# An RWKV attention and MLP kernel: small matmuls moved to quarters of the TensorE array, and a state without zero blocks

## The chip, the cores and the metric

The kernel runs on one core of a Trainium2 chip. The core has a matrix engine (TensorE, PE in the profile, with its weight loads listed as PEld), VectorE (DVE), ScalarE (ACT), GpSimd (POOL) and SyncE (SP), which issues all of this kernel's data transfers. The metric is device time of one execution in microseconds; lower is better.

TensorE multiplies a stationary operand, which is loaded into the array first, with a moving operand that streams through it. The array has 128 rows (the contraction) and 128 columns (the output's partitions). An operand that is smaller can use a part of it: the row part follows from the partitions on which the operands lie, the column part from the output's partitions. The profile writes this as rows*columns: `64*128` is a half with 64 rows, `128*64` a half with 64 columns, `64*64` a quarter.

## The reference

An RWKV-6 attention with a decay of its own for every step and channel, then an MLP with a squared ReLU. Batch 4, 8 heads, 768 steps, head size 48; model size 384, hidden size 2048. All inputs and the output are float32.

```python
for t in range(S):
    cur = np.einsum('bhd,bhe->bhde', u[None] * kt, vt)
    y[:, :, t] = np.einsum('bhd,bhde->bhe', rt, state + cur)
    state = wt[:, :, :, None] * state + np.einsum('bhd,bhe->bhde', kt, vt)
...
x = attn_out.transpose(0, 2, 1, 3).reshape(B * S, H * D)
h = x @ w_in
out = np.maximum(h, 0.0) ** 2 @ w_out
```

## The kernel before

**Tiling.** The sequence of a batch is cut into three steps of 256 positions, so there are 12 steps `s`. A step holds two chunks `c` of 128 positions. Partition `c*64 + p` holds positions `2p` and `2p+1` of chunk `c`; the two are called `j` = 0 and 1. The 8 heads go in 4 pairs `p`, with `e` = 0 or 1 for the head in the pair. A head's 48 channels are padded to 64, so that a pair fills 128 partitions after a transpose.

**Attention in a step.** `ww_`, `lw_`, `cum_`, `exp_` build the decays; `ac_` (L298) writes each chunk's whole decay to `ac_buf`; `rd_` (L305) multiplies r and k by decays into `rdec_buf`; `tr_` and `rkt_` transpose them on TensorE into `rkT`, or `dtr_` does it by a DMA. Then:

- `p_` (L341): scores of a chunk, k against r, 32 matmuls on 64x64 quarters of the array, one for each pair, chunk, head and `js`; `pm_` (L351, L354) masks them into `pmT`.
- `su_` (L371): what a chunk adds to the state, k times v. A matmul takes two heads at once, 128 columns by 96, so half of its output is a product of one head's k with the other head's v and is not wanted.
- `ts_` (L379, L381): adds the old state to it, from PSUM to `t_state`, 384 elements a partition, on DVE or ACT.
- `sn_` (L386): multiplies by the chunk's decay on POOL and writes the new bf16 state `S`. Its factor `ac_buf` holds zeros for the unwanted head of each partition, so the unwanted blocks of `S` become zero.
- `y_` (L408): masked scores times v, 32 matmuls of 48 columns with 64 rows and 128 columns of the array.
- `yq_` (L416): adds the bonus term. `vq` (v times a scalar for each position and head, made by `vq_` on POOL) is added through `spread`, an identity put in one half of 128 columns for each `j`.
- `yc_` (L422): r times the carried state, 128 rows by 64 columns of the array, 96 columns of `S` for a head pair. The zero blocks let one matmul serve two heads. In a batch's first step the first chunk has no state to carry.
- `ysb_` and `yt_`/`xt_` or `dyt_`: copy y out of PSUM and transpose it for the MLP.

`y_`, `yq_` and `yc_` accumulate in the same two PSUM banks, one for each chunk `c`, through the helper `y_mm` (L394), which is why all three have line L394 in the profile. `yy_(s)` runs `su_(s+1)`, `y_(s)`, `yq_(s)`, `yc_(s)` in a row on TensorE. In a batch's last step `su_` makes the first chunk's part alone.

**MLP.** `m1_` (L464): 6 matmuls of 256 columns for each of 8 groups; `rl_` (L473, L475) takes the ReLU; `sq_` (L481, L483) squares; `m2_` (L489): 16 matmuls of 384 columns for each chunk; `os_` (L496, L498) and `store` bring the result out.

**Order.** The order on every engine is written out by hand in the string `ORDER` (L17 to L86): each word names an operation, its step, the PSUM bank after a colon and the engine after `=` (V is DVE, A is ACT, G is POOL). Every engine runs its part of that list in order. The MLP of earlier steps is interleaved with the attention of later ones. TensorE begins with `warm_` matmuls, whose results are not used, and `constants()` (L210) fills masks, `ident`, `spread` and the zeros of `ac_buf` and `lw_buf`, mostly on POOL.

## Time and profile before

| | |
|---|---|
| three executions | 188.93, 189.06, 189.28 us; median 189.06 |
| span of the profiled execution, first to last instruction | 186.7 us; its own whole time is not listed apart from the three |
| PE busy | 177.0 us, 2303 matmuls |
| DVE, ACT, POOL busy | 125.8, 125.1, 104.9 us |
| `m1_`, L464 | 576 matmuls, 74.3 us |
| `m2_`, L489 | 384 matmuls, 71.9 us |
| `su_`, L371 | 160 matmuls of 96 columns, 6.2 us |
| `y_`, L394 | 384 of 48 columns, 7.1 us |
| `yq_`, L394 | 48 of 384 columns, 6.0 us |
| `yc_`, L394 | 160 of 96 columns, 5.7 us |
| `p_`, L341 | 384 of 128 columns on quarters, 8.2 us |
| `ts_` on DVE, L381 | 16 of 546 ns |
| `sn_` on POOL, L386 | 20 of 935 ns, median 836 |
| `ac_` on ACT, L298 | 24 of 173 ns |

Matmuls are pipelined and those on different parts of the array overlap, so a group's time is best read from the starts of its first matmul and of the next group's. "Idle" in the profile is time in which an engine had nothing running, with the instruction that ended it; "issue" is time in which it waited for nothing that the profile shows. The granted clock of TensorE was 0.999 of full speed.

### The profile page before, as it was taken

The numbers are of one execution on the slowest core, as the hardware profiler recorded it, in microseconds if no ns is written. First come the engines' busy times: TensorE is split into PE (matmuls) and PEld (weight loads), VectorE is DVE, ScalarE is ACT, GpSimd is POOL, SyncE is SP. The second block draws the span as 40 slices with busy tenths as digits, with TensorE's granted clock in tenths as the row PEclk, the third lists the DMA queues.
The fourth block names the chain that finished last, engine by engine and source line by source line (L and its number), as shares of the span: only waits on it lengthen the run. The fifth ranks groups of instructions, "written<-read, shape, count | busy, mean of one in ns | idle before, by whom it ended". The sixth has DMA issues, their size and how long they took to land.

```text
span 186.7 us, 5422 instructions
## 1 busy us (share of the span) xinstructions
PE 177.0 (95%) x2303; PEld 125.4 (67%) x2303; DVE 125.8 (67%) x170; ACT 125.1 (67%) x205; POOL 104.9 (56%) x99
## 2 busy tenths in 40 slices
PE   7686998999999999999999999999999999999992
PEld 2344587766777777777776766777666777776761
DVE  4379979686799876983849699795946472562020
ACT  5278978889659795797687577968541656156732
POOL 7289627695897998959496981563934130000000
PEclk9999999999999999999999999999999999999999
DMA  6999999999999999979999999890539150203022
GB/s 151 269 274 341 330 280 381 340 280 264 275 234 218 257 239 236 248 148 147 279 185 260 220 270 251 240 147 32 66 63 201 30 172 0 46 0 126 4 84 84
DMA packets 78952, 35.81 MB, mean 192 GB/s; under 512 B 72144, under 2 KB 77392, under 8 KB 78928
## 3 DMA queue, kind: packets, MB, share of 16 engines
q1 hardware_dynamic: 78928, 35.46, 82.5%
q8 instruction: 18, 0.29, 0.7%
q14 instruction: 6, 0.05, 0.1%
HBM read 25.36 MB, written 4.72 MB: 161 GB/s over the span
## 4 chain that ended last, share of the span: by engine, by line
PE 80%; DVE 8%; ACT 5%; issue 3%; DMA 3%; SPq 0%; ACTq 0%
PE m L464 32%; PE bk L489 31%; PE att L394 8%; DVE rdec_buf L305 4%; PE att L341 3%; PE att L371 3%; DMA w_raw<-in_w_dram 3%; PE bk L444 1%; PE att L286 1%; PE att L287 1%; ACT att L291 1%; DVE r_raw L256 1%; ACT ac_buf L298 1%; DVE pmT L351 1%; DVE pmT L354 1%
## 5 line engine op out<-in xcount | busy, mean ns | idle before, releaser
L464 PE MATMUL m<-xT,wi_sb 128*128 128x256 bf16 x576 | 74.3, 273 | 0.5 <-ACT gt L473 0.5
L489 PE MATMUL bk<-wo_sb,gt 128*128 128x384 bf16 x384 | 71.9, 326 | 0.0
L464 PEld LDWEIGHTS <-wi_sb 128*128 128x128 bf16 x576 | 54.9, 98 | 13.9 <-issue 1.4
L473 ACT ACTIVATE gt<-m 128x512 f16<-128x512 f32 x68 | 39.7, 596 | 34.4 <-PE m L464 34.1
L489 PEld LDWEIGHTS <-gt 128*128 128x128 bf16 x384 | 36.9, 98 | 19.3
L481 ACT ACTIVATE gt<-gt 128x1024 bf16<-128x1024 f16 x36 | 37.6, 1053 | 0.9 <-DVE gt L475 0.7
L354 DVE TENSOR_TENSOR pmT<-att,mask 128x1024 bf16<-128x1024 f32 x22 | 26.3, 1218 | 5.6 <-PE att L341 5.5
L386 POOL TENSOR_TENSOR S<-t_state,ac_buf 128x384 bf16<-128x384 f32 x20 | 18.7, 935 | 19.9 <-DVE t_state L381 13.2
L475 DVE TENSOR_SCALAR gt<-m 128x512 f16<-128x512 f32 x28 | 19.2, 687 | 14.6 <-PE m L464 11.9
L264 POOL TENSOR_TENSOR ku<-k_raw,u_bc 128x768 f32<-128x768 f32 x12 | 22.5, 1878 | 9.1 <-DVE q L273 4.7
L269 POOL TENSOR_TENSOR ku<-ku,r_raw 128x768 f32<-128x768 f32 x12 | 22.9, 1910 | 1.0 <-DMA r_raw<-in_r_dram 0.8
L277 POOL TENSOR_TENSOR vq<-v_raw,q 128x768 bf16<-128x768 f32 x12 | 18.2, 1520 | 9.1 <-DVE q L273 4.8
L305 DVE TENSOR_TENSOR rdec_buf<-r_raw,att 128x768 bf16<-128x768 f32 x12 | 11.3, 952 | 3.8 <-ACT att L291 2.2
L498 DVE TENSOR_SCALAR o_sb<-bk 128x384 f32<-128x384 f32 x11 | 6.1, 551 | 11.0 <-PE bk L489 11.0
L291 ACT ACTIVATE att<-att 128x768 f32<-128x768 f32 x12 | 9.4, 795 | 3.7 <-PE att L287 3.6
L305 DVE TENSOR_TENSOR rdec_buf<-k_raw,att 128x768 bf16<-128x768 f32 x12 | 11.4, 947 | 0.5 <-ACT ac_buf L298 0.5
L506 PE MATMUL bk<-warm 128*128 128x512 bf16 x35 | 10.5, 452 | 1.2 <-DVE half_ones L212 1.2
L273 DVE TENSOR_REDUCE q<-ku 128x16 f32<-128x768 f32 x12 | 11.3, 943 | 0.0
L496 ACT ACTIVATE o_sb<-bk 128x384 f32<-128x384 f32 x13 | 6.4, 490 | 6.2 <-PE bk L489 6.2
L483 DVE TENSOR_TENSOR gt<-gt 128x1024 bf16<-128x1024 f16 x12 | 8.9, 753 | 2.0 <-ACT gt L473 2.0
L381 DVE TENSOR_TENSOR t_state<-S,att 128x384 f32<-128x384 bf16 x16 | 8.7, 546 | 1.8 <-PE att L371 1.8
L247 ACT ACTIVATE lw_buf<-ww 128x384 bf16<-128x384 f32 x12 | 6.2, 524 | 5.3 <-DVE ww L243 5.3
(72 smaller groups left out, 179.8 us busy)
## 6 DMA issues: line engine op xcount, KB each, us to landing
w_raw<-in_w_dram SPq DMA_DIRECT2D x12, 384.0 KB, 5.1
k_raw<-in_k_dram SPq DMA_DIRECT2D x12, 384.0 KB, 6.1
r_raw<-in_r_dram SPq DMA_DIRECT2D x12, 384.0 KB, 6.2
v_raw<-in_v_dram SPq DMA_DIRECT2D x12, 384.0 KB, 6.0
out_dram<-o_sb SPq DMA_DIRECT2D x24, 192.0 KB, 3.1
w_st<-in_moe_w_in_dram SPq DMA_DIRECT2D x4, 768.0 KB, 8.5
w_st<-in_moe_w_out_dram SPq DMA_DIRECT2D x4, 768.0 KB, 8.7
rkT<-rdec_buf SPq DMA_TRANSPOSE x16, 4.0
```

The costliest lines, as they stand in the source:

```text
L264: nc.gpsimd.tensor_mul(ku[:], raw["k", s][:, :, 1:3, :], u_bc[:, :, None, :].to_broadcast([C, H, 2, D]))
L269: nc.gpsimd.tensor_mul(ku[:], ku[:], raw["r", s][:, :, 0:2, :])
L277: nc.gpsimd.tensor_mul(vq[:].rearrange("p j h d -> p h j d"), raw["v", s][:], tiles.pop(("q", s))[:, :, :, None].to_broadcast([C, H, 2, D]))
L305: nc.vector.tensor_mul(rdec[:, i, :, :, 0:D], x.rearrange("p h j d -> p j h d"), cs[:, i, 0:DM].rearrange("p (h d) -> p h d", h=H)[:, None ...
L354: nc.vector.tensor_mul(pmT, ps_p[:].rearrange("p e (a x) -> p (e a) x", a=2), mk.to_broadcast([C, 4, 2 * C]))
L386: nc.gpsimd.tensor_mul(t[:], tiles.pop(("ts", s, c))[:].rearrange("p (a e d) -> p a e d", a=HP, e=2), tiles["a_c", s][:, :, c, :, None].to ...
L394: nc.tensor.matmul(ps_y[rows, c, cols], lhsT, rhs, start=fresh, stop=True, skip_group_check=True)
L464: nc.tensor.matmul(ps1[:, j, :], wi_sb[:, n // 4, kk, n % 4 * 128:(n % 4 + 1) * 128], tiles["xT", s][:, :, kk, :], start=(kk == 0), stop=( ...
L473: nc.scalar.activation(rl, m1, AF.Relu, scale=RS)
L475: nc.vector.tensor_scalar(out=rl, in0=m1, scalar1=RS, scalar2=0.0, op0=ALU.mult, op1=ALU.max)
L481: nc.scalar.activation(gt, rl, AF.Square)
L489: nc.tensor.matmul(m2, gt[:, n, c * C:(c + 1) * C], wo_sb[:, n, :], start=(n == 0), stop=(n == NT - 1))
```

## The change

- The state has 48 columns for a head pair instead of 96: partitions 0 to 63 hold head `e` = 0 of each pair, 64 to 127 head `e` = 1, and there are no zero blocks. `t_state` and `S` are half as wide, `ac_buf` too; it needs no zeros, and `ac_` is one activation on all 128 partitions.
- `su_` makes one matmul for each head, on a quarter of the array: rows by chunk `c`, columns by `e`, 48 columns moving. 32 matmuls instead of 16.
- `y_` splits its 128 output positions into `j` = 0 and 1, each on a quarter: 64 matmuls instead of 32, still 48 columns.
- `yq_` uses quarters of `ident` for `spread`, which is gone: 4 matmuls with a different quarter each, 384 columns.
- `yc_` makes a matmul for each head. First the half with `e` = `c`, on quarters: 16 matmuls of 48 columns. Then the half with `e` = 1 - `c`, on tiles of 64 rows and 32 columns of the array: 32 matmuls of 48 columns. In the first half, as in `y_`, rows from half `c` of the array write chunk `c`'s bank; in the second they write the other one.
- `ORDER` is unchanged. PE gets 3167 matmuls instead of 2303.

```diff
-    spread = consts.tile([C, 2, C], BF16)
...
-    ac_bufs = [consts.tile([C, HP, 2, 2], FP32, name=f"ac_buf{i}") for i in range(NAC)]
+    ac_bufs = [consts.tile([C, HP, 2], FP32, name=f"ac_buf{i}") for i in range(NAC)]
...
-        for t in ac_bufs:
-            nc.gpsimd.memset(t[:], 0.0)
-        nc.gpsimd.memset(spread[:], 0.0)
         for c in range(2):
             rows = slice(c * Q, (c + 1) * Q)
-            for j in range(2):
-                nc.gpsimd.tensor_copy(spread[rows, j, j * Q:(j + 1) * Q], ident[rows, rows])
...
-        for e in range(2):
-            rows = slice(e * DP, (e + 1) * DP)
-            nc.scalar.activation(
-                a_c[rows, :, :, e], cs[rows, 0, DM:DM + 2 * HP].rearrange("p (a c) -> p a c", c=2), AF.Exp)
+        nc.scalar.activation(a_c[:], cs[:, 0, DM:DM + 2 * HP].rearrange("p (a c) -> p a c", c=2), AF.Exp)
...
-                    part = slice(c * Q, (c + 1) * Q)
-                    nc.tensor.matmul(ps_su[c][:, p * 2 * D:(p + 1) * 2 * D],
-                                     rdec[part, 1, j, 2 * p:2 * p + 2, :], v_bf[part, 2 * p:2 * p + 2, j, :],
-                                     start=(j == 0 and p == 0), stop=(j == 1), skip_group_check=True)
+                    for e in range(2):
+                        part, rows, h = slice(c * Q, (c + 1) * Q), slice(e * DP, (e + 1) * DP), 2 * p + e
+                        nc.tensor.matmul(ps_su[c][rows, p * D:(p + 1) * D], rdec[part, 1, j, h, :],
+                                         v_bf[part, h, j, :], start=(j == 0 and p == 0), stop=(j == 1),
+                                         skip_group_check=True)
...
-        ts = tiles["ts", s, c] = a_mid.tile([C, DM], FP32, name="t_state")
+        ts = tiles["ts", s, c] = a_mid.tile([C, HP * D], FP32, name="t_state")
...
-        t = tiles["S", s + c, 1 - c] = a_mid.tile([C, HP, 2, D], BF16, name="S", bufs=6)
+        t = tiles["S", s + c, 1 - c] = a_mid.tile([C, HP, D], BF16, name="S", bufs=6)
...
+    def y_mm(s, c, rows, cols, lhsT, rhs):
+        fresh = (s, c, rows.start // Q) not in begun
+        begun.add((s, c, rows.start // Q))
+        nc.tensor.matmul(tiles["y", s][rows, c, cols], lhsT, rhs, start=fresh, stop=True, skip_group_check=True)
...
-                        y_mm(s, c, slice(h * D, (h + 1) * D),
-                             pmT[part, p // 2, 2 * e + p % 2, js, :], v_bf[part, h, js, :])
+                        for j in range(2):
+                            rows = slice(j * Q, (j + 1) * Q)
+                            y_mm(s, c, rows, head(h), pmT[part, p // 2, 2 * e + p % 2, js, rows], v_bf[part, h, js, :])
...
-        for j in range(2):
-            for c in range(2):
-                part = slice(c * Q, (c + 1) * Q)
-                y_mm(s, c, slice(0, DM), spread[part, j], vq[part, j].rearrange("p h d -> p (h d)"))
+        for c in range(2):
+            part = slice(c * Q, (c + 1) * Q)
+            for j in range(2):
+                y_mm(s, c, slice(j * Q, (j + 1) * Q), slice(0, DM), ident[part, part],
+                     tiles["vq", s][part, j].rearrange("p h d -> p (h d)"))
...
-        for c in range(0 if s % NB else 1, 2):
-            for p in range(HP):
-                for j in range(2):
-                    y_mm(s, c, slice(2 * p * D, (2 * p + 2) * D),
-                         tiles["rkT", s][:, 0, j, p, c * Q:(c + 1) * Q],
-                         tiles["S", s, c][:, p].rearrange("p e d -> p (e d)"), j)
+        rT = tiles["rkT", s][:, 0]
+        for e_is_c, n in (True, Q), (False, Q // 2):
+            for p in range(HP):
+                for c in range(0 if s % NB else 1, 2):
+                    e = c if e_is_c else 1 - c
+                    rows = slice(e * DP, (e + 1) * DP)
+                    for j in range(2):
+                        for t0 in range(0, Q, n):
+                            y_mm(s, c, slice(j * Q + t0, j * Q + t0 + n), head(2 * p + e),
+                                 rT[rows, j, p, c * Q + t0:c * Q + t0 + n], tiles["S", s, c][rows, p, :])
```

More of the change, by code (lines that the diff above doesn't have):

```diff
@@ L369, in su_ @@
                 for c in range(n_c):
-                    part = slice(c * Q, (c + 1) * Q)
-                    nc.tensor.matmul(ps_su[c][:, p * 2 * D:(p + 1) * 2 * D],
-                                     rdec[part, 1, j, 2 * p:2 * p + 2, :], v_bf[part, 2 * p:2 * p + 2, j, :],
-                                     start=(j == 0 and p == 0), stop=(j == 1), skip_group_check=True)
+                    for e in range(2):
[3 more added lines that the diff above has]
+                                         skip_group_check=True)
     def ts_(s, c):
-        ps_su = tiles["su", s][c][:, 0:DM]
-        ts = tiles["ts", s, c] = a_mid.tile([C, DM], FP32, name="t_state")
+        ps_su = tiles["su", s][c][:, 0:HP * D]
+        ts = tiles["ts", s, c] = a_mid.tile([C, HP * D], FP32, name="t_state")
         if s % NB == 0 and c == 0:
@@ L380, in ts_, with head @@
         else:
-            nc.vector.tensor_add(ts[:], tiles["S", s, c][:].rearrange("p a e d -> p (a e d)"), ps_su)
+            nc.vector.tensor_add(ts[:], tiles["S", s, c][:].rearrange("p a d -> p (a d)"), ps_su)
     def sn_(s, c):
-        t = tiles["S", s + c, 1 - c] = a_mid.tile([C, HP, 2, D], BF16, name="S", bufs=6)
-        nc.gpsimd.tensor_mul(t[:], tiles.pop(("ts", s, c))[:].rearrange("p (a e d) -> p a e d", a=HP, e=2),
-                             tiles["a_c", s][:, :, c, :, None].to_broadcast([C, HP, 2, D]))
-    def y_mm(s, c, cols, lhsT, rhs, j=None):
-        ps_y = tiles["y", s]
-        rows = slice(0, C) if j is None else slice(j * Q, (j + 1) * Q)
-        fresh = (s, c) not in begun
-        begun.add((s, c))
-        nc.tensor.matmul(ps_y[rows, c, cols], lhsT, rhs, start=fresh, stop=True,
-                         skip_group_check=True)
-    begun = set()
+        t = tiles["S", s + c, 1 - c] = a_mid.tile([C, HP, D], BF16, name="S", bufs=6)
+        nc.gpsimd.tensor_mul(t[:], tiles.pop(("ts", s, c))[:].rearrange("p (a d) -> p a d", a=HP),
+                             tiles["a_c", s][:, :, c, None].to_broadcast([C, HP, D]))
+    begun = set()
+    def head(h):
+        return slice(h * D, (h + 1) * D)
+    def y_mm(s, c, rows, cols, lhsT, rhs):
+        fresh = (s, c, rows.start // Q) not in begun
+        begun.add((s, c, rows.start // Q))
+        nc.tensor.matmul(tiles["y", s][rows, c, cols], lhsT, rhs, start=fresh, stop=True, skip_group_check=True)
     def y_(s):
@@ L407, in y_ @@
                         part = slice(c * Q, (c + 1) * Q)
-                        y_mm(s, c, slice(h * D, (h + 1) * D),
-                             pmT[part, p // 2, 2 * e + p % 2, js, :], v_bf[part, h, js, :])
+                        for j in range(2):
+                            rows = slice(j * Q, (j + 1) * Q)
+                            y_mm(s, c, rows, head(h), pmT[part, p // 2, 2 * e + p % 2, js, rows], v_bf[part, h, js, :])
     def yq_(s):
-        vq = tiles.pop(("vq", s))
-        for j in range(2):
-            for c in range(2):
-                part = slice(c * Q, (c + 1) * Q)
-                y_mm(s, c, slice(0, DM), spread[part, j], vq[part, j].rearrange("p h d -> p (h d)"))
+        for c in range(2):
[3 more added lines that the diff above has]
+                     tiles["vq", s][part, j].rearrange("p h d -> p (h d)"))
     def yc_(s):
-        for c in range(0 if s % NB else 1, 2):
+        rT = tiles["rkT", s][:, 0]
+        for e_is_c, n in (True, Q), (False, Q // 2):
             for p in range(HP):
-                for j in range(2):
-                    y_mm(s, c, slice(2 * p * D, (2 * p + 2) * D),
-                         tiles["rkT", s][:, 0, j, p, c * Q:(c + 1) * Q],
-                         tiles["S", s, c][:, p].rearrange("p e d -> p (e d)"), j)
+                for c in range(0 if s % NB else 1, 2):
[5 more added lines that the diff above has]
+                                 rT[rows, j, p, c * Q + t0:c * Q + t0 + n], tiles["S", s, c][rows, p, :])
     def yy_(s):
```

## Prediction

> **What bounds the kernel now.** I read the page's totals first, then the chain of work that ended last, then busy time by stage, then the timeline of one attention step on TensorE (PE).

> ```profile
> PE 177.0 (95%) x2303; PEld 125.4 (67%) x2303; DVE 125.8 (67%) x170; ACT 125.1 (67%) x205; POOL 104.9 (56%) x99
> ...
> PE 80%; DVE 8%; ACT 5%; issue 3%; DMA 3%; SPq 0%; ACTq 0%
> PE m L464 32%; PE bk L489 31%; PE att L394 8%; DVE rdec_buf L305 4%; PE att L341 3%; PE att L371 3%; DMA w_raw<-in_w_dram 3%; PE bk L444 1%; PE att L286 1%; PE att L287 1%; ACT att L291 1%; DVE r_raw L256 1%; ACT ac_buf L298 1%; DVE pmT L351 1%; DVE pmT L354 1%
> ```

> PE is busy for 95% of the span and holds 80% of the chain. The lines that change, L394 and L371, hold 11%, about 20 us; that is all there is to win or multiply. By stage:

> ```profile
> 0.00:20.00 20.00, 14.85 (x176) 7.55 (x176) 13.28 (x22) 12.05 (x25) 14.67 (x30) 1.00 1.01 263
> 20.00:33.00 13.00, 12.43 (x190) 9.44 (x187) 11.69 (x19) 10.78 (x17) 6.49 (x6) 1.00 1.08 333
> 33.00:60.00 27.00, 26.86 (x384) 19.39 (x382) 20.91 (x29) 21.58 (x34) 22.08 (x17) 1.00 1.18 267
> 60.00:90.00 30.00, 30.00 (x433) 22.17 (x432) 23.05 (x31) 23.05 (x41) 25.86 (x21) 1.00 1.02 215
> ```

> PE is the second column. From 33 us on it never really rests, with DVE and ACT (fourth and fifth) at 77%. So PE's own time is the price there, and only before 33 us do other engines set the pace. One attention step (columns: start, length, line, output<-inputs, shapes, count):

> ```profile
> 83.45 0.51 PE L371 MATMUL att<-v_bf,rdec_buf 64*128 64x96 bf16 x16
> 83.80 0.56 PE L394 MATMUL att<-v_bf,pmT 64*128 64x48 bf16 x32
> 84.20 0.48 PE L394 MATMUL att<-vq,spread 64*128 64x384 bf16 x4
> 84.62 0.53 PE L394 MATMUL att<-S,rkT 128*64 128x96 bf16 x16
> 85.08 0.28 PE L464 MATMUL m<-xT,wi_sb 128*128 128x256 bf16 x1
> ...
> 88.13 0.64 PE L341 MATMUL att<-rkT 64*64 64x128 bf16 x32
> 88.70 0.28 PE L464 MATMUL m<-xT,wi_sb 128*128 128x256 bf16 x1
> ```

> Lengths overlap, so starts are the measure: `su_` 0.35 us, `y_` 0.40, `yq_` 0.42, `yc_` 0.46. Single records within them: `su_` issues pairs (two row halves, 3 ns apart) every 42.5 ns, `y_` every 25 ns, `yq_` 160 ns, `yc_` 42.5 ns. The last row pair is the nearest row to what is new: `p_` already runs on 64x64 quarters, four matmuls at once 3 ns apart, a set every 56 ns for 128 columns. A change of array shape costs the rest: from the last matmul's final column to the next one's first I get 0.11 us at `yq_` to `yc_`, 0.11 at `yc_` to `m1_`, 0.11 at `p_` to `m1_`.

> **The change, part by part.** *Pace of a 48-column quarter set.* Not in the trace. In `p_` the second load of a quarter's 64 weight columns starts 28 ns after the first, so a load takes about 28 ns; it runs beside the set's 56 ns of streaming. At 48 columns (20 ns) the load is longer than the stream. I take 30 ns a set: the load plus the 2 ns by which it trails its set's first matmul. Lower bound 25 ns (the 48-column pairs of `y_`, the shortest pace shown); upper bound 48 ns, load and stream in turn, which `p_` speaks against.

> In `su_` the second load of 128 columns starts only 15 ns after the first. [...]

> *`su_`:* 16 matmuls of 96 columns become 32 of 48, 8 sets: 8 x 30 = 0.24 us for 0.34, -0.10. Where only one state is needed (`s` = 2, 5, 8, 11) 8 become 16, still 8 sets, -0.10.
> *`y_`:* 32 become 64, 16 sets: 0.48 for 0.40, +0.08. No columns are saved; pairs become fours.
> *`yq_`:* four matmuls of 384 columns, two after two, become one set: 0.16 for 0.32, -0.16.
> *`yc_`:* 16 become 16 quarters (4 sets, 0.12 us) and 32 tiles of 64x32 (4 sets of eight). A pair of instructions, load and matmul, goes out every 3.3 ns in `p_`, so eight need 27 ns: 0.11 us. Together 0.23 for 0.34, -0.11. Where only the second chunk is carried (`s` = 0, 3, 6, 9) it was 0.17: +0.06. Eight tiles at once are not in the trace; below, 25 ns a set; above, two at a time as in `y_`, 100 ns, which is +0.29 us a step, +3.5 in all.
> *Shape changes:* before, three in a step (full to 64x128, to 128x64, to full); after, three (full to 64x64, to 64x32, to full): nothing, by the 0.11 rows within 0.01 of each other. In step 0 `p_` stands between `y_` and `yq_`, and two changes fall away; ACT's cast and copy at 20.59 cover it.

> Sum on PE: 8 steps at -0.10 + 0.08 - 0.16 - 0.11 = -0.29, four at -0.12: -2.8 us.

> *Other engines.* `ts_` halves: 384 elements take 546 ns, the 768 of L305 950, so 192 come to about 345, 0.2 less for each of 20. `sn_` on POOL halves from 836 ns to about 430. Both hide under PE, and only keep DVE and POOL level with a shorter PE. `ac_` goes from two activations of 173 ns to one; in the chain at 30.0 both stand before ACT's square and `rl_`: -0.18. At 9.46 they stand before `exp_`; a gain of up to 0.35 starts there, but ACT's wait for `v_raw`, which lands at 18.77, takes most of it back. The POOL fills and copies of `spread` and `ac_buf` (3.6 to 5.0 us) lie ahead of a wait for `u` until 8.4: nothing. `vq_` and `v_` are as before, and no wait or DMA is added. So -2.8 - 0.2 = -3.0.

> Not all of that will show: at 83.44 `su_` starts 60 ns after the `rd_` it needs, so a quicker PE meets DVE there. I keep 85%: -2.5. The span was 186.7; the three times are 188.93 to 189.28, their median 189.06, 2.4 above it, and I leave those 2.4 as they are. Forecast **186.5 us**; with sets at 25 ns and all kept, 184.4; with a fifth kept, 188.5.

> **Rivals.**
> *B, instructions come too slowly: slower.* The step now sends 148 loads and 148 matmuls (132 where `s`+1 has one state, 124 where `s` carries one), 296 instructions in 0.24 + 0.48 + 0.16 + 0.23 + 0.11 = 1.22 us: 4.1 ns each. Before it sent 136 in 1.52 us, 11.2 ns each. The fastest long stretches shown are 64 in 0.40 (`y_`, 6.3 ns) and 96 in 0.74 (`su_` and `y_`, 7.7 ns); both are paced by the array, so the supply may be quicker, but nothing shows it. It decides from 1.52 us / 296 = 5.1 ns. Over a batch's three steps the instructions are 248, 264, 296 and the old times 1.35, 1.52, 1.52: at 6.3 ns the kernel loses 2.7 us (191.8), at 7.7 7.3 (196.4), at 11.2 18.6 (207.7). For it: 1728 more PE instructions (4608 to 6336), all in dense bursts. Against it: within a set instructions stand 1.7 ns apart, and no slowing is seen towards the end of 32 `y_` pairs. Chance 0.29.
> [...]
> *C, the gain is eaten.* PE reaches `su_`, `p_` and the `m1_` banks earlier and waits for DVE or ACT: within 0.2% of 189.06 (what this measurement can tell from no change). For: the 60 ns above, and 77% on DVE and ACT. Against: ACT waited 34.1 us for L464, so it mostly runs behind PE with time in hand, and DVE and POOL are relieved. Chance 0.06.
> *D, a quarter's load does not hide behind its 20 ns stream.* 28 sets at 48 ns, +0.50 us a step, +6.0: 189.06 + 6.0 - 3.0 = 192.1. The eight tiles in pairs would be 189.6 after the same sum. Against: `p_`, 56 ns a set with 28 ns loads inside. Chance 0.08.
> That quarters do not run at once at all is excluded by `p_`.

> **How the numbers follow.** Forecast 0.57, B 0.29, C 0.06, D 0.08. So faster 0.57, same 0.06, slower 0.37. The forecast's own range is 184.4 to 188.5; to leave out no more than 2 in 10 the range has to take in C, D and the nearer half of B: 184.4 to 200.

> **What would show it.** Right: starts of `su_`, `y_`, `yq_`, first and second half of `yc_`, `m1_` at 0.24, 0.48, 0.16, 0.23 and 0.23 (each half of `yc_` with one shape change); sets of four with 3 ns inside; `ts_` near 345 ns, `sn_` near 430. Wrong by B: even spacing of single matmuls in `y_` and `yc_`, 13 ns or more, with gaps that end in "issue". Wrong by C: new PE idle time put down to DVE or ACT. Wrong by D: 48 ns between sets.

## The result and the profile after

The changed kernel takes 199.45 us (median of four, 198.52 to 201.21) against 189.01 for the kernel before: a ratio of 1.054, interval 1.047 to 1.062. It is slower, where faster was forecast. In what follows, a time is the median of all executions, and a ratio leaves out those that took over 1.5% longer than the shortest of the same kernel. The profiled execution of the changed kernel took 198.52 us with a span of 196.7, 10.0 more than before. From its page, and below it the one line of the page before that is compared:

```profile
PE 179.6 (91%) x3167; PEld 128.7 (65%) x3167; DVE 127.0 (65%) x170; ACT 121.5 (62%) x193; POOL 96.4 (49%) x90
...
PE   7876579999989999999969999699999999999993
...
PEclk9999879999999999999999999969999999999999
...
q8 instruction: 24, 0.39, 0.9%
...
PE 78%; DVE 8%; issue 6%; DMA 3%; SPq 2%; ACT 1%; DVEq 0%
```

```profile
q8 instruction: 18, 0.29, 0.7%
```

PE is idle for 17 us instead of 10. No other engine explains that: DVE is 1.2 us busier than before, ACT and POOL are less busy. And "issue", time for which the profile names no cause, doubles from 3% to 6% of the chain. Two places have a lower granted clock. One more figure has moved: the queue that brings instructions has 24 transfers (0.39 MB) where it had 18 (0.29 MB).

The attention step itself did become shorter. PE's timeline of the step that starts at 83.45 in the kernel before:

```profile
88.64 0.44 PE L363 MATMUL att<-v_bf,rdec_buf 64*64 64x48 bf16 x32
88.92 0.71 PE L389 MATMUL att<-v_bf,pmT 64*64 64x48 bf16 x64
89.45 0.35 PE L389 MATMUL att<-vq,ident 64*64 64x384 bf16 x4
89.62 0.56 PE L389 MATMUL att<-S,rkT 64*64 64x48 bf16 x48
90.11 0.50 PE L463 MATMUL m<-xT,wi_sb 128*128 128x256 bf16 x3
```

By starts: `su_` 0.28 us for 0.35, `y_` 0.53 for 0.40, `yq_` 0.17 for 0.42 (its shape change is gone), `yc_` 0.49 for 0.46; 1.47 for 1.63. The time is lost elsewhere, in a few pieces. The chain of work that ended last (start, length, what):

```profile
20.05 0.16 PE att L389 x3
20.21 2.44 issue
22.65 0.65 PE att L389 x24
...
26.24 0.63 PE att L389 x23
26.87 1.43 issue
28.30 0.51 PE att L389 x22
...
97.54 1.05 PE att L389 x91
98.59 1.65 issue
...
125.50 0.76 PE m L463 x6
126.26 2.05 issue
128.31 0.81 PE bk L488 x4
```

PE stops for some 1.5 to 3 microseconds: within `yq_` of step 0, within `y_` of step 1, within `yc_` at 98, and between `m1_` and `m2_` at 126, where the instructions were not even changed. A fifth stop of 0.6 us is in `cum_` at 113. The `m1_` and `m2_` matmuls are the same 960 in both kernels, so the starts of some of them tell where the changed kernel falls behind (us, from the two traces; the matmuls are counted from 0):

```
matmul of the 960      before    after   behind by
first, m1_ of step 0     23.39    28.74    5.35   stops of 2.77 and 1.65
112                      41.15    46.24    5.09
342                      85.08    90.11    5.04   three attention steps, 0.11 to 0.19 saved in each,
                                                  less 0.44 for a wait for a copy of rkT
388                      93.53   100.36    6.82   stop in yc_
472                     107.26   114.52    7.27   stop in cum_
536                     118.86   125.43    6.58   a wait for DVE at 112 is shorter, two steps save
542                     119.52   128.31    8.79   stop ahead of m2_
564                     122.35   132.81   10.46   half clock
780                     158.41   168.48   10.07   two steps save 0.26 and 0.13
```

From the last start before each stop to the first one behind it, the five stops come to 9.2 us. Behind the two longest the clock falls. Busy time by stage (length, PE, PEld, DVE, ACT, POOL, granted clock, DMA share, GB/s):

```profile
122.00:126.00 4.00, 4.00 (x171) 3.27 (x170) 3.02 (x6) 2.90 (x6) 0.83 (x2) 1.00 1.20 311
126.00:128.30 2.30, 0.26 (x3) 0.09 (x1) 1.93 (x3) 1.86 (x3) 2.30 (x2) 1.00 0.77 195
128.30:131.50 3.20, 3.19 (x16) 1.99 (x16) 0.52 (x1) 0.60 (x1) 2.18 (x2) 0.67 0.83 172
131.50:135.00 3.50, 3.50 (x54) 2.67 (x52) 1.81 (x2) 1.55 (x3) 0.00 (x0) 0.82 0.10 25
```

The clock's records say it exactly: half speed from 129.4 to 132.8 and from 23.6 to 27.0, 3.4 us each. The first of these costs 1.7 us by the table above. The other may account for much of the 0.9 us that the first stage lost beyond its two stops; no run shows it alone.

```
kernel    block end   PE stops at   transfer         PE goes on   after its end
changed         449        19.89    19.87 -  21.13        22.65        1.53
changed         705        26.65    25.66 -  26.82        28.30        1.48
changed        3521        98.41    97.54 -  98.72       100.25        1.52
changed        4033       113.47   111.54 - 112.60       114.11        1.51
changed        4545       125.99   125.73 - 127.10       128.31        1.22
before          449            -    19.59 -  20.80        22.44        1.64   no stop; the nearest of its 18
```

Here "block end" is the number of the first instruction of the next block, and the last column is the time from the transfer's end to that instruction's start.

**Theory F:** PE uses up a block before the next one has come, because the 296 instructions of a step pass in about 1.4 us (1.35 in the step shown). **Theory O:** the stops belong to the new operations (changes of array shape, banks written from two row halves), and the grid of 256 is chance.

### The profile page after: what moved, and what is told of

Its sections match the earlier page's. It is cut to its first block, busy times and chain, and to the rows that moved or that the text cites. A ratio compares the mean times of both kernels' runs of the same rounds, so it can differ in the third digit from the quotient of the medians.

```text
span 196.7 us, 7127 instructions
## 1 busy us (share of the span) xinstructions
PE 179.6 (91%) x3167; PEld 128.7 (65%) x3167; DVE 127.0 (65%) x170; ACT 121.5 (62%) x193; POOL 96.4 (49%) x90
## 4 chain that ended last, share of the span: by engine, by line
PE 78%; DVE 8%; issue 6%; DMA 3%; SPq 2%; ACT 1%; DVEq 0%
PE bk L488 31%; PE m L463 31%; PE att L389 7%; DMA r_raw<-in_r_dram 3%; DVE rdec_buf L296 3%; PE att L332 3%; PE att L363 2%; PE bk L443 1%; SPq L161 1%; DVE ww L237 1%; PE att L280 1%; DVE r_raw L250 1%; PE att L281 1%; PE bk L505 1%; SPq L189 1%
## 5 line engine op out<-in xcount | busy, mean ns | idle before, releaser
L463 PE MATMUL m<-xT,wi_sb 128*128 128x256 bf16 x576 | 75.4, 275 | 0.3 <-ACT gt L472 0.2
L463 PEld LDWEIGHTS <-wi_sb 128*128 128x128 bf16 x576 | 55.5, 99 | 15.6 <-issue 3.4
L271 POOL TENSOR_TENSOR vq<-v_raw,q 128x768 bf16<-128x768 f32 x12 | 17.7, 1477 | 16.9 <-DVE q L267 13.4
L378 POOL TENSOR_TENSOR S<-t_state,ac_buf 128x192 bf16<-128x192 f32 x20 | 11.4, 571 | 29.5 <-DVE t_state L373 20.8
L482 DVE TENSOR_TENSOR gt<-gt 128x1024 bf16<-128x1024 f16 x12 | 10.8, 907 | 3.7 <-ACT gt L472 3.7
L505 PE MATMUL bk<-warm 128*128 128x512 bf16 x35 | 11.6, 490 | 1.2 <-DVE half_ones L211 1.2
L389 PE MATMUL att<-v_bf,pmT 64*64 64x48 bf16 x768 | 9.1, 190 | 2.8 <-issue 1.4
L435 ACT CAST y_sb<-att 128x768 bf16<-128x768 f32 x9 | 7.2, 796 | 5.5 <-PE att L389 2.9
```

Source lines behind the costliest of these rows:

```text
L271: nc.gpsimd.tensor_mul(vq[:].rearrange("p j h d -> p h j d"), raw["v", s][:], tiles.pop(("q", s))[:, :, :, None].to_broadcast([C, H, 2, D]))
L389: nc.tensor.matmul(tiles["y", s][rows, c, cols], lhsT, rhs, start=fresh, stop=True, skip_group_check=True)
L463: nc.tensor.matmul(ps1[:, j, :], wi_sb[:, n // 4, kk, n % 4 * 128:(n % 4 + 1) * 128], tiles["xT", s][:, :, kk, :], start=(kk == 0), stop=( ...
L505: nc.tensor.matmul(bk[i][:], warm[:, 0:C], warm[:], start=True, stop=True)
```

## The experiments

**The same work, 128 instructions later.** In `warm_`:

```diff
+        if n == 16:
+            for _ in range(80):
+                nc.tensor.matmul(bk[i][:, 0:102], warm[:, 0:C], warm[:, 0:102], start=True, stop=True)
+            return
```

> The changed kernel with its first 16 warm-up matmuls of 512 columns made as 80 of 102: the same columns, 64 more loads and 64 more matmuls (128 PE instructions) ahead of everything else. Theory F (instructions are fetched in blocks of 256, and PE stops where a block ends before the next is there; in the changed kernel all five stops fall on instruction 449 + 256 k, counted from the span's start): the stops stay on the count 449 + 256 k and so fall on other work. [...] Time 195 to 201 us. Theory O (the stops belong to the new operations and their places, such as shape changes or PSUM banks): the stops stay in yq_ of step 0, y_ of step 1, behind yc_ at 98 and before m2_ at 126, 128 instructions later in the count, and the time stays at 199.5.

204.1 us in its one run. The stops are at instructions 705, 961, 1729, 2241, 2753 and 3265: again all on 449 + 256 k, and none of the old places has one (449 passes without a stop, and the work that had been at 3521, 4033 and 4545 runs through). They last 3.7, 1.8, 3.8, 1.5, 1.2 and 0.7 us. The chain around 1729, now in `yc_` at 57:

```profile
55.71 0.37 PE att L363 x32
56.08 1.04 PE att L389 x111
57.12 3.65 issue
60.77 0.23 PE att L389 x3
```

The author's estimate of how late a block comes, which no trace shows, gave 2.6, 1.8 and 2.4 us at 1729, 2753 and 3265; they came out as 3.8, 1.2 and 0.7, and 705, 961 and 2241 were not in it. The time is above what F expected. Half clock for 10.2 us followed the stops at 705 and 961, and for 6.8 us the one at 1729; the expectation had not counted that. O falls: the same operations in the same order stop elsewhere.

**Fewer instructions in a step.** `y_` on halves again, ahead of `su_`:

```diff
-                        for j in range(2):
-                            rows = slice(j * Q, (j + 1) * Q)
-                            y_mm(s, c, rows, head(h), pmT[part, p // 2, 2 * e + p % 2, js, rows], v_bf[part, h, js, :])
+                        y_mm(s, c, slice(0, C), head(h), pmT[part, p // 2, 2 * e + p % 2, js, :], v_bf[part, h, js, :])
...
+        y_(s)
         if s + 1 < NS:
             su_(s + 1)
-        y_(s)
```

> The changed kernel with y_ back on 64x128 halves (32 matmuls for 64) and ahead of su_, so that one more change of array shape is needed in a step. A step sends 232 instructions for 296. [...] With 0.15 to 0.25 us a step kept: 185.5 to 188.5 us. Theory O: the quarters of su_, yq_ and yc_ and the 64x32 tiles are all still there, so most of the stops are too: 195 us or more.

192.88 us, 1.022 of before (1.016 to 1.029): some 60% of the loss goes with 64 of 296 instructions. The stops that are left are at 449 (1.5 us), 705 (0.6) and 1473 (0.9), the grid once more, none after 57 us. The expectation of 185.5 to 188.5 counted, by that estimate, on at most one stop, ahead of 33 us. What it lacked, besides the two further stops, is 3.4 us of half clock at 21.8, and a wait of 1.25 us until 34.6, where DVE is late with `rd_`: one multiply, `k_raw`, took 2.17 us from 31.54 on instead of 0.55, while POOL's `ku_` ran from 31.16 to 33.28. In the kernel before, `k_raw` was done by 29.04 and `ku_` began at 30.73. Whether the stops brought the two together is not shown: they also overlap in a kernel without such a stop (the kernel before, shifted, further down).

**Fewer other transfers.** Inputs of steps 4 to 11 not loaded; those steps compute with the inputs of steps 0 to 3 again, so their output is another:

```diff
+        if s >= 4:
+            raw[part, s] = raw[part, s - 4]
+            return
```

> The changed kernel with r, k, v and w loaded for steps 0 to 3 alone; steps 4 to 11 compute with those again, so their part of the output is another. PE's instructions are the same ones in the same order; two thirds of the input transfers are gone. Theory F with a block's transfer queued behind the inputs' transfers: stops at instructions 449 and 705 stay (2.8 and 1.7 us, all loads are still there), those at 3521, 4033 and 4545 (1.8, 0.6, 2.3 us) shrink to 1 us or less in sum of each or go, 194 to 197 us. Theory F with a latency of its own, whatever else is transferred: the five stops keep their sizes within 0.3 us, 199 us.

192.98 us in its one run, below both expected ranges. The stops at 449 and 705 stay, 2.6 and 1.2 us; those at 3521 and 4033 are gone; that at 4545 is 1.6 for 2.3, where 1 us or less was expected. In sum the stops are 3.8 us shorter. The half clock behind the last one, 1.7 us above, does not come either; together that is the 5.5 us by which the span is shorter. In the chain:

```profile
97.04 1.05 PE att L392 x92
98.08 1.42 PE m L466 x12
...
122.34 0.76 PE m L466 x6
123.10 1.34 issue
124.44 0.81 PE bk L491 x4
```

PE reached the block end at 3521 at 97.9 and its transfer had ended at 95.96, where in the changed kernel the two were at 98.41 and 98.72. So how late a block is depends on what else is in transit. In the first stage, where the loads are dense and were all kept, both stops stayed. With a third of the traffic gone the fastest burst still overtook one block.

**One part alone.** The kernel before with `yq_` on quarters:

```diff
+                y_mm(s, c, slice(0, DM), ident[part, part], vq[part, j].rearrange("p h d -> p (h d)"), j)
```

> The kernel before with yq_ alone on quarters, and nothing else changed (no instruction more on PE). 0.16 us less of columns in a step, one more change of array shape at 0.11: 12 x -0.05 = -0.6, 188.4 us, no stop of PE over 1 us after 33 us (theory F: no instruction is added). Theory O (a quarter's pass into both banks at once makes stops): stops in yq_, above 190.

188.27 us, 0.998 of before (0.995 to 1.001), so not settled by the times alone. In the trace each step is 0.04 us shorter at PE, where 0.05 was expected, and there is no such stop: quarters that write both banks at once do not make one.

**Can a shift save the kernel with halves?** Three phases of it, 32, 64 and 112 instructions later, by splitting the warm-up as above into 32, 48 and 72 matmuls.

> The kernel with y_ on halves (192.9) and 32 PE instructions more ahead, by the same split of the warm-up. Theory F: the stops at 449 (1.5 us), 705 (0.6) and 1473 (0.9) move to other work; with 6 to 8 us from the point at which a block's successor is asked for to its use, one of about 1.4 us is left at 705 and none later: 188.5 to 191.5 us. Theory O: 192.9 within 0.5.

> The same with 64 instructions more ahead. Theory F: one stop of about 1.5 us at 705, in m1_ behind step 0, and none later: 188.5 to 191.5 us. Theory O: 192.9 within 0.5.

> The same with 112 instructions more ahead. Theory F: one stop of about 1.3 us at 705, in y_ of step 1, none at 449: 188.5 to 191.5 us. Theory O: 192.9 within 0.5.

192.37 (1.014, 1.008 to 1.020), 193.33 (1.019, 1.013 to 1.025) and 192.32 us (1.013, 1.008 to 1.019): none reached what F expected, and by its time alone the second fits O as well. The places decide: the stops did move along the grid: at 449 (1.2 us) and 1473 (1.3) with 32; at 705 (1.1), 1473 (0.5) and 4033 (1.9) with 64; at 705 alone (2.7) with 112; holds of up to 0.33 us at block ends are left out. (The trace of the first is of its slowest execution, 194.70 us.) But there was always at least one, half clock of 3.4 to 6.8 us fell into the first 33 us in each, and the wait for `rd_` at 34 to 38 us was there each time, 1.2 to 1.9 us. A phase only chose which burst was hit. No run shows when a block is asked for, so the 6 to 8 us in the first of the three expectations are an estimate without a measurement; what the traces show in its place is the transfer, of 0.9 to 2.6 us, and the 1.2 to 1.6 us from its end until PE goes on after a stop.

**The kernel before, shifted.** Only the split of the warm-up, 128 instructions.

> The kernel before, with nothing changed but its first 16 warm-up matmuls of 512 columns, which become 80 of 102: 128 more PE instructions in a stretch in which PE waits for its first input anyway. No quarter and no 64x32 tile is added. Theory F (blocks of 256 instructions end at 449 + 256 k): with the shift the block that ends at 705 ends within yq_ and yc_ of step 1, some 2 us ahead of its successor: one stop of 1 to 2.5 us at instruction 705, ended by a transfer of 16 KB that closes some 1.4 us before; 189.8 to 191.5 us. Theory O (the stops belong to the new operations): no stop, 189.0 within 0.3.

190.29 us, 1.006 of before (1.002 to 1.010). That is the forecast time, but not by the forecast cause: the stop at 705 did not come, since the block's transfer had ended 1.89 us before PE reached it. F's mechanism is neither shown nor refuted by that; its forecast of where a block comes late was wrong here. The trace, of the slowest of the ten executions (192.03 us), has half clock from 20.4 to 23.9, with no block end there, and the 2.2 us `k_raw` multiply with a wait of 2.1 us behind it. Eight of the ten had a mean clock of 0.998 or more, so the half clock does not explain the median. A shift alone cost 1.2 us; from what, stays open.

**Instructions alone, no new operation.** The kernel before, `y_` of two steps cut into columns of 8:

```diff
+                        n = 8 if s in (5, 8) else D
+                        for d in range(0, D, n):
+                            y_mm(s, c, slice(h * D + d, h * D + d + n),
+                                 pmT[part, p // 2, 2 * e + p % 2, js, :], v_bf[part, h, js, d:d + n])
```

> The kernel before with y_ of steps 5 and 8 alone cut finer: each of its 32 matmuls of 48 columns becomes 6 of 8 columns with a weight load each, on the same 64x128 halves: 160 matmuls and 160 loads more in each of the two steps. No quarter and no 64x32 tile anywhere. At 25 ns for a pair of row halves, as before, the array needs 2.0 us more in each step. Theory F: a block of 256 instructions begins and ends inside each of these bursts, so PE stops once in y_ of step 5, at instruction 2497 (449 + 256 x 8), and once in or just behind y_ of step 8, at 3521 or 3777, for 2.5 to 4.5 us each: 198 to 203 us. Theory O (new operations make the stops): no stop, 193 us.

204.95 us in its one run. Two stops, at 2497 and 3777, both named ahead, 3.0 us each:

```profile
86.82 2.73 PE att L394 x194
89.55 2.68 issue
92.23 1.26 PE att L394 x17
...
126.73 2.26 PE att L394 x178
128.99 2.83 issue
131.82 1.85 PE att L394 x31
```

Their transfers ran from 89.85 to 90.83 and from 129.44 to 130.43, and PE went on 1.40 and 1.39 us after the end. Behind each stop comes half clock for 6.8 us. By the 1.7 us for 3.4 above that is an estimated 3.4 us each, which was not in the range. No quarter and no 64x32 tile is in this kernel beyond those of `p_`. F stands.

**Both kernels' best.** Steps 0 to 2 as before (the changed kernel stops in steps 0 and 1, at 449 and 705), from step 3 on with `y_` on halves:

```diff
+                    if s < NB:
+                        part = slice(c * Q, (c + 1) * Q)
+                        nc.tensor.matmul(ps_su[c][:, p * 2 * D:(p + 1) * 2 * D],
...
+        if s < NB:
+            su_(s + 1)
         y_(s)
-        if s + 1 < NS:
+        if NB <= s < NS - 1:
             su_(s + 1)
```

> Steps 0 to 2 as in the kernel before; steps 3 to 11 as in the kernel with y_ on halves and ahead of su_ (state without zero blocks, su_, yq_ and half of yc_ on quarters, the other half on 64x32). [...] From step 3 on the other kernels showed 0.08 to 0.2 us less in each step; a stop of up to 1 us at one place is possible. 186.5 to 188.5 us. Theory O: stops wherever quarters and 64x32 tiles are used, above 189.

No stop and full clock throughout, and a span of 185.8 us in the profile, 0.9 under before; each step from 3 on is 0.09 to 0.22 us shorter, against three short waits of 0.3 to 0.4, and one wait, at 113 in the kernel before, is 0.7 shorter. The ten executions spread from 186.98 to 190.89, median 189.50, above the expected range; the ratio, without the two longest, is 0.998 (0.993 to 1.003). It removes the loss of the change and is not shown to beat the kernel before.

## Why the prediction was wrong

- **The views of the kernel before** were read rightly as far as they went: PE is the bound, and L371 and L394 hold what there is to win. The 18 instruction transfers on its page enter no term.
- **Pace of a quarter set, 30 ns:** 31.7 ns in the first 130 instructions or so of a burst. (Its 20 ns for 48 columns are `yq_`'s 160 ns for 384.) Rival D's 48 ns and eight tiles in pairs did not come; tiles of 64x32 mostly start 3.3 ns apart, as forecast.
- **The sum, -0.29 or -0.12 a step, -2.8:** measured 0.08 to 0.26, some 0.16 in the step shown. The sets cost 2 ns more than taken, and from about the 130th instruction of a burst on matmuls start 8.3 ns apart, a set in 33 ns. With a load to each matmul that is 4.2 ns an instruction, which looks like the supply that rival B asked about; no run isolates it. It lies under B's 5.1 ns, so B as an even pace did not decide.
- **The step that failed is "no wait or DMA is added".** The instructions are themselves transfers: six more of 16 KB, each needed at a block end. The kernel before came as near as 1.64 us to the first of them; the change sends a block's worth of instructions in about the time that one transfer takes (1.2 us), and five of the 24 came too late: 9.2 us. A shift, a lower count, fewer other transfers, and instructions without new operations all moved the stops as this says.
- **Half clock** stands in no term: 3.4 us twice, at a price of 1.7 us for the one that can be read alone.
- **"Wrong by B"** named even spacing of single matmuls, 13 ns or more, with gaps that end in "issue". Both are there, but the spacing is 8.3 ns and costs little, and the gaps come at ends of blocks of 256, not throughout. B had the right resource and the wrong form.
- **Other engines:** `ts_` took 345 ns, as worked out. `sn_` took 508 ns at its median, not 430. `ac_`'s 0.18 and the head's 0.35 cannot be seen under the stops.
- **Range:** 199.45 lies just inside 200, on the side that was given 0.37. That is luck: the upper part of the range was B's even pace, which did not decide, and the stops and the half clock stood in no term.

## What to carry to other kernels

Before a change that makes many small matmuls of few large ones, count PE's instructions per microsecond in the burst, not only its columns. Here 256 instructions in a row took 3.99 us at least in the kernel before and as little as 1.16 us in the changed one. In the twelve traces a block's transfer began at most 295 instructions ahead of its use and took 0.9 to 2.6 us. Compare each instruction transfer's end with the time at which PE reaches the block's end: every stop ended 1.2 to 1.6 us after its transfer did, and where PE reached the block's end 1.61 us or more after the transfer there was no stop. The kernel before already showed a margin of 1.64. Here long gaps marked "issue" that lay whole blocks of 256 instructions apart were this, wherever in the code they fell.

## What was not expected of the hardware

- After a stop PE went on only 1.2 to 1.6 us after the last packet of its instruction block; what passes in that time no run shows.
- A block's transfer starts up to 3.9 us after PE has begun the block before it in the changed kernel, in the first stage, where loads are dense (up to 5.6 in the kernel before, shifted). Behind 45 us it was up to 2.6 us, and without most of the input loads at most 1.9.
- Deep in a burst, from about its 130th instruction on, PE started a matmul and its load every 8.3 ns (the changed kernel, step at 88.64 us); before that, and for the first 25 or so of the 64x32 tiles behind it, they started as little as 3.3 ns apart.
- After stops of about 2.3 us and more the granted clock was at half for 3.4 us or a multiple of it (3.4, 6.8, 10.2); after the stops of 1.83 and 0.64 us in the changed kernel it was not. That is no threshold: with `y_` on halves, half clock began at 21.8 us beside a stop of 1.5 us, and at 20.8 beside one of 1.2 with 32 instructions more.
- Open: why the 1.4 us wait for `pmT` at 17.5 us, which all kernels have, is followed by half clock in the shifted kernel and not in the one before, and what makes the hybrid's executions spread by 4 us.
